# Attention and a gated feed-forward: loads of q and k for two head pairs at a time, output rows stored whole, and a new order

## The chip, the cores and the metric

The kernel runs on one core of a Trainium2 chip. The core has five engines that run programs of their own and meet at semaphores: TensorE (PE in the profile; its weight loads are listed apart as PEld), VectorE (DVE), ScalarE (ACT), GpSimd (POOL) and SyncE (SP), which here only issues DMAs. The metric is the device time of one execution in microseconds; times of a kernel are the median of several runs. A page of the profile and a trace show one more execution, instruction by instruction.

## What is computed

Attention with RMS-normalised q and k over 8 batches of 12 heads (sequence 448, head size 64), then for each batch a feed-forward block with a gate that comes from a convolution along the sequence:

```python
q_n, k_n = rmsnorm(q, g_q), rmsnorm(k, g_k)          # x / sqrt(mean(x*x) + 1e-6) * g
scores = np.matmul(q_n, k_n.transpose(0, 1, 3, 2)) / sqrt(64)
attn = np.exp(scores - scores.max(-1)); attn /= attn.sum(-1) + 1e-9
x = np.matmul(attn, v)                               # (8, 12, 448, 64) -> (8, 448, 768)
h = np.maximum(x @ w_in, 0.0)                        # w_in 768 x 1024
conv_out = sum(conv_w[k] * hp[:, k:k + S] for k in range(3))   # hp: h padded by one row
gate = 1.0 / (1.0 + np.exp(-conv_out))
out = (h * gate) @ w_out                             # w_out 1024 x 768
```

All inputs and outputs are float32. The large products are made of float16 parts: each operand is split into a high and a low half, and three products (high x high, high x low, low x high) are added up in a bank of PSUM.

## The kernel before

**Tiling.** The 96 heads are worked in 48 pairs (n = 0 to 47, six pairs make a batch). For a pair the q and k rows lie in a buffer `qk0`, `qk1` or `qk2` (`qkbuf`, L169): 128 partitions x (q, k) x 2 heads x 4 row blocks x 64 numbers. The steps of a pair are: `load_k` (L358, two DMAs) and `load_q` (L369, one DMA) from HBM; `square` (L375, on ScalarE as L378 or on POOL as L95); `square_sum` (VectorE); `rsqrt` (L406 to L440, on VectorE or POOL, for two pairs in one step from pair 2 on: `duo(n)` at L402 gives the first of the two and their number); `apply_rms` (`sq<-qk,st`, L95); then `qk_transpose` on TensorE (L494) or `x_turn` by DMA, and the split into halves; `scores` (L673, matmuls with 64 rows); `soft_max` and `soft_exp` (L688); the split of the probabilities into a high half (L83) and a low half, `p_lo` (`ph<-e,ph`, L95, on VectorE or POOL); `p_turn` (L726, DMA transposes issued by SyncE; the first ten pairs are turned on TensorE); `pv` (L824, weights of 64 columns). Row sums are turned by a small matmul (L755), stored to DRAM and loaded back as a broadcast (`rB`, L774), by which `x_scale` (L831) divides. v is split likewise: `v_hi`, and `v_lo` at L801, which only VectorE does. L83, L87, L89 and L95 are lines of helpers through which the steps copy, scale and combine.

**The feed-forward.** When a batch's six pairs are done, `in_part` (L898) multiplies x by w_in for each of 8 blocks of 128 hidden units, `in_relu`, `in_conv` (L926) and `in_gate` (L936) follow, the result is split into `gring` (NGR = 13 slots; with slots in the freed weight tiles NGS = 16), and `out_part` (L977) multiplies by w_out, per chunk of 128 rows (`ch`) and half of 384 columns (`half`). `out_evac` (L982) moves a half from PSUM into a tile of the pool "c", and `out_store` (L991) stores that half, 192 KB. The weights are split in the first 130 us, block by block: `rest` makes the low halves, on POOL with two instructions (L314, L315) or on VectorE with one (L317).

**Order.** Nothing runs in the order of the source. Every step is written as a function, planned at a time (`at(...)`, `plan_qk`, `plan_moe` ...), and at build time a list scheduler puts all steps of all engines in one order: `needs` says which steps must come before, `options` which engines may do a step and how long each takes, `takes` and `vacant` which tile it holds, and the numbers in `PH` (L20) set due times and priorities (`p_lo` for the step p_lo, `nl` for how many hidden blocks of the last batch start early, `nbulk` for how many large loads may be under way). So the choice of engine for a step (`on[...]`) comes out of it too. Where a step waits is decided by the semaphores that follow from this order.

Buffers (`BUFS`, L106): 3 of q and k, 12 of `x`, 3 of `c` (hidden values in conversion and output halves), 2 of `rB`, and 8 banks of PSUM shared by scores, transposes and matrix sums. The three buffers of q and k are single pairs: `load_k(n)` needs the normalisation of pair n - 3.

Of the kernel before, what the change touches and what calls it, by code (L numbers as in the profile page):

```python
# [20 lines left out]
    T0=11.0, N0=5, T=16.382, ti=26.404, si=4.968, so=8.766, hop=0.561, beta=0.03, wi0=-36.475,  # L21
    wi1=117.871, wo0=26.473, wo1=140.589, cw=-9.12, tg=-80.448, tl=37.151, ea=0.984, te=114.439,
    ep=0, hs=0, nf=3, adj=0.197, nz=8, ne=0, sc=5, tc=2, mc=9, p_qe=0.915, p_evac=0.829,
    p_hi=1.186, p_lo=6.193, p_rms=1.69, p_v=0.867, p_x=0.082, p_g=2.32, p_relu=0.547, p_cv=1.114,
    p_qz=0.74, p_ev=5.993, sp=0.148, nbulk=6, p_rs=0.05, p_sq=0.891, p_w=0.552, v0=-6.388, dg=7,
    n1=10, sw=0.0, nl=3, tj=-0.029, hk=0, pvs=1, pk=0.1, p_sa=0.167, p_ph=0.412, p_pl=0.72, nq=3,
    nk=92, p_qh=0.575, p_ql=0.384, tq=10.598, ti0=0.04, ti1=0.124, ti2=-0.224, ti3=0.742,
    ti4=0.066, ti5=-0.171, ti6=0.596, ti7=0.034, si0=0.995, si1=1.598, si2=1.683, si3=1.424,
    si4=1.633, si5=1.152, si6=1.198, si7=1.044, to0=0.237, to1=0.161, to2=-0.044, to3=0.013,
    to4=0.226, to5=-0.711, to6=-0.117, to7=0.325, so0=1.431, so1=1.535, so2=1.849, so3=1.519,  # L30
    so4=2.126, so5=1.521, so6=1.163, so7=0.964,
# [23 lines left out]
def tile_attention_moe(ctx: ExitStack, tc, q, k, v, g_q, g_k, w_in, conv_w, w_out, out):  # L55
# [41 lines left out]
    def move(e, dst, src):  # L97
# [9 lines left out]
        qkf=3, sq=2, st=2, qT=2, kT=2, qz=2, v=4, sst=6, e=2, PT=2, x=12, c=3,  # L107
        rB=2, vacc=2, vsc=4, cwb=3, s=PH["sc"], t=PH["tc"], m=PH["mc"], rd=2, rsum=2, rT=1, mx=10, ph=3, vp=2,
# [60 lines left out]
    qkbuf = [const.tile([P, 2, 2, 4, D], F32, name=f"qk{i}") for i in range(BUFS["qkf"])]  # L169
# [6 lines left out]
    NGR = 13  # L176
# [180 lines left out]

    def load_k(n):  # L358
        ring = rings.setdefault("qkf", Ring(BUFS["qkf"]))
        x = ring.put(("qkf", n), qkbuf[ring.count % BUFS["qkf"]])  # L360
        rows = slice(n * 2 * S, (n + 1) * 2 * S)
        src = kf[rows].rearrange("(h k) d -> h k d", h=2)
        for i, m in enumerate((4, 3)):
            queue("lk").dma_start(
                x[HALF[i], 1, :, :m],
                src[:, 256 * i : 256 * i + 64 * m].rearrange("h (p t) d -> p h t d", t=m),
            )

# [71 lines left out]
    def apply_rms(n, i):  # L440
# [5 lines left out]
            old("qkf", n)[:m, i], y.unsqueeze(3).to_broadcast([m, 2, NB, D]), ALU.mult,  # L446
# [96 lines left out]
    def plan_qk(n):  # L543
        s = base(n)
        lead = PH["tl"] if n else 60.0
        at(s - lead, load_k, n)
        at(s - lead, load_q, n)
# [434 lines left out]
    def out_evac(b, ch, half):  # L982
        sc = old("vsc", b - 1)[:, 5:6] if b % 2 == 1 and ch == 0 else old("vsc", b)[:, 4:5]
        o = new("c", ("o", b, ch, half), [P, S], F32)
        copy_scaled(
            on["out_evac", b, ch, half], o[:, :NO2], bank("m", ("o", b, ch, half))[:, :NO2], sc
        )

    def out_store(b, ch, half):
        row0 = out_place(b, ch)[1]  # L990
        queue("out").dma_start(  # L991
            outf[row0 : row0 + P, half * NO2 : (half + 1) * NO2],
            old("c", ("o", b, ch, half))[:, :NO2],
        )

    def plan_moe(b):
# [25 lines left out]
        for i, (ch, half) in enumerate(units):  # L1022
# [4 lines left out]
            at(u + so + 2.0, out_store, b, ch, half)  # L1027
# [17 lines left out]
    def prepare():  # L1045
# [705 lines left out]
```

## Time and profile before

| | us |
|---|---|
| three runs | 892.53, 888.18, 892.11 |
| median | 892.11 |
| the profiled execution: its time | 887.41 |
| the profiled execution: its span (first to last instruction) | 885.6 |
| mean granted clock of TensorE | 0.984 of full speed |

| engine | busy us | share of the span | instructions |
|---|---|---|---|
| TensorE, matmul | 817.3 | 92% | 5416 |
| TensorE, weight load (beside) | 417.8 | 47% | 5416 |
| VectorE | 721.8 | 81% | 1189 |
| ScalarE | 677.3 | 76% | 1474 |
| POOL | 603.0 | 68% | 744 |

A group of instructions is named by its line, engine, operation and tiles: `sq<-qk` is an instruction that reads q and k and writes the squares. In a list of single instructions the first number is the start in us from the span's begin, the second the duration, and in brackets stands the idle time of the engine before it with the instruction that ended it. All sums below are made against the profiled execution, 887.41, and then put on the median.

### The profile page before, as it was taken

To read this page: it belongs to the slowest core of one execution; us is meant where nothing else is said; L and a number is where in the kernel's file an instruction comes from. 1 tells how busy PE (TensorE), PEld (TensorE's weight loads), DVE (VectorE), ACT (ScalarE), POOL (GpSimd) and SP (SyncE) were. 2 spreads that over 40 slices of the span, in tenths; PEclk is the share of its full clock that TensorE was granted. 3 is DMA by queue.
4 is the path that set the end of the run, shared out by engine and by line. 5 is a ranking of instruction groups with operands and counts; after the bars stand their busy time and mean duration, and the time that the engine had idled before them with its cause. 6 is when DMAs were issued, how large, how long until landed. Compare 5 with 4: busy or idle time off the path is not lost.

```text
span 885.6 us, 16303 instructions
## 1 busy us (share of the span) xinstructions
PE 817.3 (92%) x5416; PEld 417.8 (47%) x5416; DVE 721.8 (81%) x1189; ACT 677.3 (76%) x1474; POOL 603.0 (68%) x744
## 2 busy tenths in 40 slices
PE   0588889999999799999999999998999999999998
PEld 0244444544444344455545554544455555555554
DVE  5889998889989998899888888989898788971330
ACT  1778878879988898888888878987688778783441
POOL 6238867668777977887878756887678868853120
PEclk9989999999999899999999999999899999999999
DMA  8936642128898888888998699979588888456101
GB/s 267 263 104 168 174 98 63 36 77 162 193 195 170 147 179 177 188 179 168 193 180 179 123 184 191 186 159 178 122 166 164 159 168 175 102 111 136 37 11 62
DMA packets 343585, 132.65 MB, mean 150 GB/s; under 512 B 303461, under 2 KB 341709, under 8 KB 342733
## 3 DMA queue, kind: packets, MB, share of 16 engines
q1 hardware_dynamic: 343500, 131.61, 70.3%
q8 instruction: 43, 0.70, 0.3%
q14 instruction: 42, 0.34, 0.1%
HBM read 58.22 MB, written 11.18 MB: 78 GB/s over the span
## 4 chain that ended last, share of the span: by engine, by line
PE 71%; DVE 15%; POOL 4%; ACT 4%; issue 4%; DMA 2%; SPq 1%; ACTq 0%; POOLq 0%; DVEq 0%
PE banks L977 21%; PE banks L898 20%; PE banks L673 10%; PE banks L824 9%; PE banks L494 4%; PE banks L815 3%; PE banks L735 3%; DMA qk<-in_q_dram 1%; DVE st L395 1%; ACT e L688 1%; DVE ph L95 1%; POOL ph L95 1%; PE banks L755 1%; DVE vp L801 1%; DVE kT L530 1%
## 5 line engine op out<-in xcount | busy, mean ns | idle before, releaser
L95 POOL TENSOR_TENSOR ph<-e,ph 128x768 f16<-128x768 f32 (+3 forms) x272 | 256.9, 966 | 72.3 <-ACT ph L83 56.7
L898 PE MATMUL banks<-x,wi 128*128 128x448 f16 x1152 | 253.8, 356 | 0.7 <-ACT PT L83 0.7
L977 PE MATMUL banks<-wo,gring 128*128 128x384 f16 (+1 forms) x1056 | 210.4, 328 | 0.0
L898 PEld LDWEIGHTS <-wi 128*128 128x128 f16 x1152 | 109.0, 99 | 102.3 <-issue 19.4
L977 PEld LDWEIGHTS <-gring 128*128 128x128 f16 (+1 forms) x1056 | 100.8, 99 | 74.1 <-issue 16.1
L83 ACT CAST ph<-e 128x1024 f16<-128x1024 f32 (+1 forms) x139 | 129.4, 931 | 5.3 <-DMA PT<-ph 3.5
L673 PE MATMUL banks<-kT,qT 64*128 64x448 f16 x864 | 107.2, 362 | 8.2 <-DVE qT L532 4.7
L95 POOL TENSOR_TENSOR sq<-qk,st 112x512 f32<-112x512 f32 (+1 forms) x85 | 94.4, 1127 | 23.1 <-DVE st L417 8.2
L824 PE MATMUL banks<-PT,vp 128*64 128x448 f16 (+1 forms) x836 | 98.2, 365 | 4.2 <-DVE c_(1_6_3089 L936 3.1
L494 PE MATMUL banks<-ident,sq 128*128 128x128 f32 (+1 forms) x364 | 61.0, 280 | 26.1 <-POOL sq L95 20.3
L395 DVE TENSOR_REDUCE st<-sq 128x16 f32<-128x1024 f32 x48 | 58.0, 1209 | 16.7 <-ACT sq L378 16.6
L494 PEld LDWEIGHTS banks<-ident,sq 128*128 128x128 f32 (+1 forms) x364 | 43.9, 144 | 53.1 <-POOL sq L95 23.2
L95 POOL TENSOR_TENSOR x<-rB,x 128x448 f16<-128x448 f32 x48 | 53.2, 1109 | 22.1 <-ACT x L83 20.8
L824 PEld LDWEIGHTS <-vp 128*64 128x64 f16 (+1 forms) x836 | 41.8, 110 | 55.0 <-issue 35.3
L673 PEld LDWEIGHTS <-qT 64*128 64x128 f16 x864 | 35.1, 95 | 64.1 <-issue 36.2
L735 PE MATMUL banks<-ident,e 128*128 128x128 f32 x280 | 45.4, 291 | 12.7 <-ACT PT L83 5.7
L378 ACT ACTIVATE sq<-qk 128x1024 f32<-128x1024 f32 x41 | 43.3, 1056 | 11.7 <-DMA qk<-in_q_dram 11.4
L831 DVE TENSOR_TENSOR rB<-banks,rB 128x448 f32<-128x448 f32 x48 | 29.7, 618 | 26.7 <-PE banks L824 20.7
L541 POOL COPY qz<-qT 64x128 f16<-64x128 f16 x86 | 32.4, 377 | 25.0 <-DVE qT L532 17.7
L977 PE MATMUL banks<-wo,wi 128*128 128x384 f16 (+1 forms) x192 | 46.9, 326 | 0.0
L735 PEld LDWEIGHTS banks<-ident,e 128*128 128x128 f32 x280 | 32.4, 146 | 29.7 <-ACT PT L83 10.6
L83 ACT COPY PT<-banks 128x512 f32<-128x512 f32 x63 | 36.0, 582 | 9.9 <-PE banks L735 9.5
(1152 smaller groups left out, 1688.8 us busy)
## 6 DMA issues: line engine op xcount, KB each, us to landing
qk<-in_q_dram SPq DMA_DIRECT2D x48, 224.0 KB
rB<-rd SPq DMA_DIRECT2D x96, 112.0 KB
qk<-in_k_dram SPq DMA_DIRECT2D x48, 128.0 KB
wo<-in_moe_w_in_dram SPq DMA_DIRECT2D x6, 1024.0 KB
v<-in_v_dram SPq DMA_DIRECT2D x24, 256.0 KB
gring<-in_moe_w_out_dram SPq DMA_DIRECT2D x8, 768.0 KB
qk<-in_k_dram SPq DMA_DIRECT2D x48, 96.0 KB
v<-in_v_dram SPq DMA_DIRECT2D x24, 192.0 KB
```

The lines of the kernel that those rows point to most:

```text
L83: (nc.scalar.copy if e == "ACT" else elementwise(e).tensor_copy)(dst, src)
L95: elementwise(e).tensor_tensor(dst, a, b, op=op)
L378: nc.scalar.activation(sq, old("qkf", n), AF.Square)
L395: nc.vector.tensor_reduce(old("st", m)[:, 0, n - m].rearrange("p i s -> p (i s)"), old("sq", n).rearrange("p i h t d -> p (i h t) d")[..., ...
L494: nc.tensor.transpose(ps[:, t * w : t * w + m], x[:m, t], ident[:m, :m])
L541: e.tensor_copy(z[HALF[h], :, HALF[h]], old("qT", n)[HALF[h], :, t0 : t0 + 64])
L673: nc.tensor.matmul(ps[u][:, :S], lhs, kt[r, w], start=(i == 0), stop=(i == 2))
L735: nc.tensor.transpose(ps[:, kt * P : (kt + 1) * P], e[:, k0 : k0 + P], ident)
L824: nc.tensor.matmul(ps[HALF[h], :S], v[:m, w, h, c % 4], pt[:m, c, h * S : (h + 1) * S], start=(i == 0), stop=(i == len(PV7) - 1),)
L831: nc.vector.tensor_tensor(t, bank("m", ("v", n))[:, :S], t, op=ALU.mult)
L898: nc.tensor.matmul(ps[:, :S], wi[:, wl, c, fc * P : (fc + 1) * P], old("x", b * NP + c)[:, xl], start=(i == 0), stop=(i == 3 * NP - 1),)
L977: nc.tensor.matmul(ps[p0 : p0 + m, :NO2], g, wo[:, wl, fc, half * NO2 : (half + 1) * NO2], start=(i == 0), stop=(i == 3 * NFC - 1),)
```

## The change

The three buffers of a single pair become two buffers of two pairs. Pairs 0 and 1 are still loaded singly; from pair 2 on one `load_k` and one `load_q` bring two pairs, 23 times. The other steps of a pair take their half of the buffer (`qk(n)`). The load of pairs n and n + 1 needs the normalisation of pairs n - 4 and n - 3.

An output chunk is gathered in one tile "o" of 768 columns (a pool with one buffer) and stored once, 384 KB.

Other buffers: `x` 12 to 10, `c` 3 to 2, `rB` 2 to 1, `gring` 13 to 12 slots. `nl` goes from 3 to 4, so that four hidden blocks of the last batch are worked while its last chunks of x are still made, and the step that writes a slot of `gring` now needs all chunks of the older batch that read the slot. The numbers of `PH` are set anew, and with them the order on all engines and the choice of engine of some steps.

```diff
-    T0=11.0, N0=5, T=16.382, ti=26.404, si=4.968, so=8.766, hop=0.561, beta=0.03, wi0=-36.475,
+    T0=11.0, N0=5, T=16.382, ti=26.404, si=4.968, so=8.925, hop=0.57, beta=0.03, wi0=-36.475,
...
-        qkf=3, sq=2, st=2, qT=2, kT=2, qz=2, v=4, sst=6, e=2, PT=2, x=12, c=3,
-        rB=2, vacc=2, ...
+        qkf=2, sq=2, st=2, qT=2, kT=2, qz=2, v=4, sst=6, e=2, PT=2, x=10, c=2, o=1,
+        rB=1, vacc=2, ...
...
-    qkbuf = [const.tile([P, 2, 2, 4, D], F32, name=f"qk{i}") for i in range(BUFS["qkf"])]
+    qkbuf = [const.tile([P, 2, 2, 2, 4, D], F32, name=f"qk{i}") for i in range(BUFS["qkf"])]
...
-    NGR = 13
+    NGR = 12
...
+    def qk_rows(x, n):
+
+        w = duo(n)[1]
+        a, b = n * 2 * S, (n + w) * 2 * S
+        return x[a:b].rearrange("(h k) d -> h k d", h=2 * w), slice(n % 2, n % 2 + w)
+
     def load_k(n):
         ring = rings.setdefault("qkf", Ring(BUFS["qkf"]))
-        x = ring.put(("qkf", n), qkbuf[ring.count % BUFS["qkf"]])
-        rows = slice(n * 2 * S, (n + 1) * 2 * S)
-        src = kf[rows].rearrange("(h k) d -> h k d", h=2)
+        if n % 2 == 0:
+            ring.put(("qkf", n // 2), qkbuf[ring.count % BUFS["qkf"]])
+        src, u = qk_rows(kf, n)
...
+    def qk(n):
+
+        return old("qkf", n // 2)[:, :, n % 2]
...
-        o = new("c", ("o", b, ch, half), [P, S], F32)
...
-    def out_store(b, ch, half):
+        if half == 0:
+            new("o", (b, ch), [P, DM], F32)
+        o = old("o", (b, ch))[:, half * NO2 : (half + 1) * NO2]
+        copy_scaled(on["out_evac", b, ch, half], o, bank("m", ("o", b, ch, half))[:, :NO2], sc)
+
+    def out_store(b, ch):
         row0 = out_place(b, ch)[1]
-        queue("out").dma_start(
-            outf[row0 : row0 + P, half * NO2 : (half + 1) * NO2],
-            old("c", ("o", b, ch, half))[:, :NO2],
-        )
+        queue("out").dma_start(outf[row0 : row0 + P], old("o", (b, ch)))
...
             pb = back(b, a[1], NGS, NFC)[0]
-            yield "out_part", pb, 3 if pb % 2 else 2, 1, 3 * NFC - 4, 4
+            for ch in range(4 if pb % 2 else 3):
+                for u in range(2):
+                    yield "out_part", pb, ch, u, 3 * NFC - 4, 4
```

What the new order looks like at three places. First SyncE's program around the loads of pairs 34 and 35, before; `qk1` takes pair 34 and `qk2` pair 35, `PT_30` to `PT_32` are the turned probabilities of pairs 30 to 32, `rd` and `rB` the row sums:

```order
L726 DMA_TRANSPOSE PT_30_5854<-ph2_73 128x7x128
L364 DMA qk1_77<-in_k_dram 64x2x256
L364 DMA qk1_77<-in_k_dram 64x2x192
L371 DMA qk1_77<-in_q_dram 112x8x64
L774 DMA rB_30_6006<-rd_30_5946 64x448 x2
...
L768 DMA rd_31_6154<-rT_31_6130 7x128
L364 DMA qk2_78<-in_k_dram 64x2x256
L364 DMA qk2_78<-in_k_dram 64x2x192
L726 DMA_TRANSPOSE PT_32_6178<-ph1_72 128x14x128
L371 DMA qk2_78<-in_q_dram 112x8x64
```

and now:

```order
L738 DMA_TRANSPOSE PT_30_5795<-ph2_73 128x7x128
L370 DMA qk1_77<-in_k_dram 64x4x256
L370 DMA qk1_77<-in_k_dram 64x4x192
L786 DMA rB_30_5945<-rd_30_5894 64x448 x2
L738 DMA_TRANSPOSE PT_31_5958<-ph0_71 128x14x128
L377 DMA qk1_77<-in_q_dram 112x16x64
```

Both pairs' rows are now asked for where pair 34's alone were, and the second group of loads, behind the sums of pair 31, is gone.

Second, TensorE around the products with v of pair 20 (weight loads and repeats are left out at the marks), before:

```order
L824 MATMUL banks_66<-PT_20_3750,vp_20_3770 64x448
...
L494 MATMUL banks_66<-ident_69,sq_22_3664 128x128 x3
...
L673 MATMUL banks_66<-kT_21_3709,qT_21_3728 128x448
...
L494 MATMUL banks_66<-ident_69,sq_22_3664 128x112 x4
...
L824 MATMUL banks_66<-PT_20_3750,vp_20_3770 64x448
...
L898 MATMUL banks_66<-x_14_2905,wi32_82 128x448
```

and now:

```order
L505 MATMUL banks_66<-ident_69,sq_22_3638 128x112 x4
...
L910 MATMUL banks_66<-x_14_2877,wi32_81 128x448
...
L685 MATMUL banks_66<-kT_21_3672,qz1_79 128x448
...
L836 MATMUL banks_66<-PT_20_3739,vp_20_3618 64x448
...
L910 MATMUL banks_66<-x_15_3054,wi32_81 128x448
```

The transposes of pair 22 and scores of pair 21, which stood between two parts of the product, now stand ahead of it, and the product is in one piece.

Third, POOL in the first 100 us, between the halves of pair 5 (`sq_5`) and its part of the rsqrt of pair 6 (`st_6`); `wi32` is w_in, `x_1` and `x_2` the results of pairs 1 and 2. Before:

```order
L95 TENSOR_TENSOR qk2_78<-sq_5_511,qk2_78 112x512
L314 TENSOR_SCALAR wi32_82<-wi32_82,wsc_86 128x1024
L315 TENSOR_TENSOR wi32_82<-wi32_82 128x1024
L95 TENSOR_TENSOR x_2_803<-rB_2_729,x_2_803 128x448
L423 TENSOR_SCALAR st_6_826<-st_6_826 128x32
```

and now:

```order
L95 TENSOR_TENSOR qk0_76<-sq_5_468,qk0_76 112x512
L314 TENSOR_SCALAR wi32_81<-wi32_81,wsc_85 128x1024
L315 TENSOR_TENSOR wi32_81<-wi32_81 128x1024
L95 TENSOR_TENSOR x_1_679<-rB_1_613,x_1_679 128x448
...
L95 TENSOR_TENSOR sq_7_809<-qk1_77 128x1024
L95 TENSOR_TENSOR x_2_825<-rB_2_738,x_2_825 128x448
...
L434 TENSOR_SCALAR st_6_815<-st_6_815 128x32
```

At the two marks stand a second and a third pair of L314 and L315 and small copies: POOL does three blocks of w_in here (two in the whole program before, one of them earlier than this) and the square of pair 7, all ahead of the rsqrt of pair 6.

## Rows read from the trace of the kernel before

**Rows 1.** Windows: start:end, length, busy us of each engine, clock, DMA share, GB/s.

```profile
0.00:140.00 140.00, 94.58 (x556) 47.73 (x557) 119.98 (x204) 95.95 (x216) 87.38 (x113) 0.97 0.66 175
80.00:100.00 20.00, 16.73 (x104) 8.18 (x104) 19.93 (x24) 18.11 (x41) 17.97 (x13) 1.00 0.61 163
140.00:660.00 520.00, 500.65 (x3349) 251.73 (x3348) 466.11 (x762) 436.75 (x955) 393.27 (x488) 0.98 0.79 160
300.00:320.00 20.00, 16.40 (x120) 8.27 (x121) 19.21 (x36) 16.77 (x36) 16.57 (x18) 0.83 0.65 142
620.00:640.00 20.00, 19.52 (x107) 8.74 (x103) 15.77 (x23) 12.36 (x28) 13.42 (x18) 0.86 0.63 127
640.00:660.00 20.00, 18.28 (x109) 9.08 (x110) 18.55 (x30) 16.73 (x35) 12.15 (x18) 0.91 0.83 174
660.00:882.00 222.00, 222.00 (x1515) 118.37 (x1513) 135.68 (x224) 144.01 (x304) 122.36 (x145) 1.00 0.55 113
```

The engines stand in the order PE, PEld, DVE, ACT, POOL, with the number of instructions in brackets.

**Rows 2.** Timeline of TensorE, 363 to 371 us: start, duration, instructions.

```profile
364.34 0.73 PE L898 MATMUL banks<-x,wi 128*128 128x448 f16 x3
365.00 1.82 PE L824 MATMUL banks<-PT,vp 128*64 128x448 f16 x16
...
369.22 0.74 PE L898 MATMUL banks<-x,wi 128*128 128x448 f16 x3
369.80 0.33 PE L977 MATMUL banks<-wo,gring 128*128 128x384 f16 x1
```

**Rows 3.** Groups by line and shape: count, then busy us, mean ns, idle before.

```profile
L317 DVE SCALAR_TENSOR_TENSOR wi<-wi,wsc 128x1024 f16<-128x1024 f32 x4 | 5.5, 1366 | 0.0
L317 DVE SCALAR_TENSOR_TENSOR wo<-wo,wsc 128x768 f16<-128x768 f32 x4 | 4.3, 1064 | 0.2 <-ACT wo L309 0.2
...
L95 POOL TENSOR_TENSOR sq<-qk 128x1024 f32<-128x1024 f32 x7 | 13.9, 1985 | 8.1 <-PE banks L494 6.7 <-issue 1.3
...
L314 POOL TENSOR_SCALAR wo<-wo,wsc 128x768 f32<-128x768 f32 x4 | 8.9, 2214 | 3.7 <-ACT wo L309 3.7
...
L315 POOL TENSOR_TENSOR wo<-wo 128x768 f16<-128x768 f32 x4 | 6.6, 1646 | 0.3
L314 POOL TENSOR_SCALAR wi<-wi,wsc 128x1024 f32<-128x1024 f32 x2 | 6.4, 3210 | 0.6 <-ACT wi L309 0.6
...
L315 POOL TENSOR_TENSOR wi<-wi 128x1024 f16<-128x1024 f32 x2 | 4.3, 2132 | 0.2
```

**Rows 4.** Timeline of TensorE at the transposes of pair 6.

```profile
108.02 0.75 PE L494 MATMUL banks<-ident,sq 128*128 128x128 f32 x4 [1.59 <-POOL sq L95]
```

**Rows 5.** Timelines around the load of q of pair 35: DMA, ScalarE, TensorE.

```profile
545.94 4.88 DMA qk<-in_q_dram
550.92 1.06 ACT L378 ACTIVATE sq<-qk 128x1024 f32<-128x1024 f32 x1 [3.63 <-DMA qk<-in_q_dram]
...
554.01 0.27 PE L755 MATMUL banks<-ident,rsum 128*7 128x128 f32 x1 [1.38 <-DVE rsum L752]
```

**Rows 6.** Line L801: min/median/max ns; then timelines of 609 to 621 us.

```profile
L801 DVE SCALAR_TENSOR_TENSOR vp<-v,vsc,vp x38: 732/747/4728, 193.9 to 790.2; 128x512 f16<-128x512 f32 x38
...
611.64 4.63 DVE L801 SCALAR_TENSOR_TENSOR vp<-v,vsc,vp 128x512 f16<-128x512 f32 x1
611.72 4.01 POOL L95 TENSOR_TENSOR ph<-e,ph 128x768 f16<-128x768 f32 x4
...
619.49 0.38 PE L755 MATMUL banks<-ident,rsum 128*7 128x128 f32 x1 [3.04 <-DVE rsum L752]
```

**Rows 7.** Timeline of 300 to 303 us, VectorE and TensorE.

```profile
300.75 1.61 DVE L432 TENSOR_TENSOR st<-st 128x32 f32<-128x32 f32 x1 [0.40 <-POOL st L430]
...
302.94 2.45 PE L824 MATMUL banks<-PT,vp 128*64 128x448 f16 x12 [3.09 <-DVE c_(1_6_3089 L936]
```

**Rows 8.** The end: timeline of ScalarE; then DMA, 882 to 886 in 40 slices.

```profile
882.19 0.58 ACT L87 ACTIVATE c_('o'_7_3_1_9926<-banks,vsc 128x384 f32<-128x384 f32 x1 [3.32 <-PE banks L977]
...
GB/s 0 0 0 0 0 0 0 0 0 0 0 0 0 0 0 0 169 384 399 338 399 231 46 0 0 0 0 0 0 0 0 0 0 0 0 0 0 0 0 0
```

More of the change, by code (lines that the diff above doesn't have):

```diff
@@ L369, in load_q @@
     def load_q(n):
-        rows = slice(n * 2 * S, (n + 1) * 2 * S)
+        src, u = qk_rows(qf, n)
         queue("lq").dma_start(
-            old("qkf", n)[:PB, 0], qf[rows].rearrange("(h t p) d -> p h t d", h=2, t=NB),
-        )
+            old("qkf", n // 2)[:PB, 0, u].rearrange("p u h t d -> p (u h) t d"),
+            src.rearrange("h (t p) d -> p h t d", t=NB),
+        )
+    def qk(n):
+        return old("qkf", n // 2)[:, :, n % 2]
     def square(n):
@@ L377, in square @@
         if on["square", n] == "ACT":
-            nc.scalar.activation(sq, old("qkf", n), AF.Square)
+            nc.scalar.activation(sq, qk(n), AF.Square)
         else:
-            binary("POOL", sq, old("qkf", n), old("qkf", n), ALU.mult)
+            binary("POOL", sq, qk(n), qk(n), ALU.mult)
     def square_half(n):
@@ L545, in plan_qk @@
         lead = PH["tl"] if n else 60.0
-        at(s - lead, load_k, n)
-        at(s - lead, load_q, n)
+        if duo(n)[0] == n:
+            at(s - lead, load_k, n)
+            at(s - lead, load_q, n)
         at(s - 24.0, square, n)
@@ L1026, in plan_moe @@
             at(u + so, out_evac, b, ch, half)
-            at(u + so + 2.0, out_store, b, ch, half)
+            if half:
+                at(u + so + 2.0, out_store, b, ch)
     def load_g(i):
@@ L1167, in needs @@
             for i in range(2):
-                m = n - BUFS["qkf"]
-                yield ("x_turn" if turned(m, i) else "apply_rms"), m, i
-            yield "load_q", n - 1
+                for m in range(duo(n)[1]):
+                    m += n - 2 * BUFS["qkf"]
+                    yield ("x_turn" if turned(m, i) else "apply_rms"), m, i
+            yield "load_q", duo(n - 1)[0]
         elif name == "load_q":
@@ L1173, in needs @@
         elif name == "square":
-            yield "load_q", n
+            yield "load_q", duo(n)[0]
             for i in range(2):
@@ L1391, in needs @@
             yield "out_scales", b
+            if a[2]:
+                yield "out_evac", b, a[1], 0
         elif name == "out_store":
-            yield "out_evac", *a
+            for u in range(2):
+                yield "out_evac", *a, u
     def back(n, g, i, m=NS):
@@ L1431, in options @@
             keep_cw=lambda: [dve(0.2), act(0.25)],
-            load_k=lambda: [dma("lk", 0.41, 2)],
-            load_q=lambda: [dma("lq", 1.36)],
+            load_k=lambda: [dma("lk", 0.41 * duo(a[0])[1], 2)],
+            load_q=lambda: [dma("lq", 1.36 * duo(a[0])[1])],
             square=lambda: [act(1.06), pool(1.9)],
@@ L1476, in options @@
             out_evac=lambda: [act(0.58), dve(0.6)],
-            out_store=lambda: [dma("out", 0.65)],
+            out_store=lambda: [dma("out", 1.3)],
             sum_transpose=lambda: [pe(0.12)],
@@ L1524, in takes @@
             return "c", [(None, ("in_lo", *a[:2]))]
-        if name == "out_evac":
-            return "c", [(None, ("out_store", *a))]
+        if name == "out_evac" and not a[2]:
+            return "o", [(None, ("out_store", *a[:2]))]
         return None, []
@@ L1586, in ends @@
             return done[p] + LAT["DMA" if d else f]["DMA" if dma else e]
-        if tag == "c":
+        if tag in "co":
             old_users = held[tag][-BUFS[tag] :]
```

35 lines of the change are left out of this document (16 added, 19 removed).

## The prediction

> **What bounds the kernel now.** I first cut the span into stretches by the view that gives every engine's busy time in a window [rows 1]. In 660–882 us TensorE is busy 222.00 of 222.00 us: nothing can be gained there except by making its own work shorter. In 140–660 it is busy 500.65 of 520, so 19.35 us are idle. In 0–140 it is busy 94.58, so 45.42 are idle, and VectorE with 119.98 is the fullest engine; in 80–100 VectorE has 19.93 of 20 and POOL 17.97. Then I followed the idle times of 140–660 back, by the timelines of single stretches. They have two sorts of cause. One is a late load: the q rows of pair 35 take 4.88 us to land, ScalarE's square behind them idles 3.63, and 3 us later TensorE idles 1.38 on a result of VectorE [rows 5]. The other is an element-wise step on VectorE that stretches while POOL works: L801 has a median of 747 ns, but at 611.64 it took 4.63 us, beside a low-half step of POOL that began at 611.72 with four instructions of 4.01 us; 8 us later TensorE idles 3.04 us [rows 6]. The same at 300.75: L432 takes 1.61 us behind POOL's half of the same pair, and TensorE idles 3.09 us at 302.94 [rows 7].
>
> Such a gap costs more than itself. The granted clock is 0.83 in 300–320, 0.86 in 620–640 and 0.91 in 640–660, each time after the gap, against 1.00 in stretches without one [rows 1]: between the two levels of 1.2 and 2.4 GHz, some of these stretches ran at the lower. At 20 us each, (0.17 + 0.14 + 0.09) x 20 = 8.0 us of full-speed time lost, with the gaps 3.09 + 3.04 = 6.1: 14.1 us hang on two places, about 7 us each.
>
> So the time is TensorE's work, plus a startup that VectorE sets, plus a few accidents between engines. The change removes no matmul; its reach is in the order, the startup, the accidents and the last store.
>
> **The change part by part**, against the profiled execution's own 887.41 us (0.53% under the median of 892.11).
>
> *TensorE's order.* The matmuls are the same in number and shape. What the order does is to set kinds apart or together: 64-row scores, 64-column PV and full 128 x 128 tiles. In the listings, shape changes along TensorE's program go from 320 to 302. A change has a small price: three in_part matmuls followed by a PV hold TensorE from 364.34 to 365.00, 0.66 us, the same three followed by an out_part of the same shape from 369.22 to 369.80, 0.58 [rows 2]. 18 x 0.08 = 1.4 us, all on the path as far as TensorE is saturated. Ends: 0 to -1.8. I take **-1.4**.
>
> *Startup.* Three `rest` steps of the weights go from VectorE to POOL: one of w_in (1.37 us) and two of w_out (1.06 each), 3.5 us off the fullest engine; POOL gets 2 x L314 + L315: 3.21 + 2.13 and twice 2.21 + 1.65, together 13.1 us [rows 3]. In the stretch 80–100 POOL has only 2 us left [rows 1]. In the order, POOL now has a third weight step and a whole square (1.99 us by [rows 3]) ahead of its part of the rsqrt of pair 6. And TensorE's transposes of pair 6 waited 1.59 us on POOL at 108.02 already before [rows 4]. So VectorE gives up to 3.5 back, and POOL may take as much: it has 7.3 us more ahead of that point (5.3 + 2.0), against the waits that it had there. Ends: -4 and +3. I take **-1.0**, nearer to VectorE's row, since it is the engine at 19.93 of 20.
>
> *Loads of two pairs.* Per two pairs, three DMA issues instead of six; SyncE has 97 issues fewer in all, and none of them was on the path. The odd pair's rows now come with the even one's, so a wait like that of pair 35 (3.63 on ScalarE, 1.38 on TensorE [rows 5]) has no place any more: its load is issued a whole pair earlier. In return the even pair waits for a transfer of twice the bytes, by [rows 5] up to 4.88 us more if the transfer is as slow as there, and the load itself must wait until both pairs of its buffer have been normalised. The even pairs' loads stood some microseconds ahead of their squares. One full gap like [rows 5] with a little low clock behind it is 2 us; there is one clear case in the trace. Ends: -4 (two such) and 0 (another wait is next behind it). I take **-2.0**.
>
> *Which engine does which element-wise step.* POOL gets nine more squares, 9 x 1.985 = 17.9 us, and the 13.1 us of `rest` [rows 3]; four more low halves of P and thirteen fewer casts about cancel. That is 31 us more on POOL, of which 18 lie in 140–660, where it is busy 393.27 of 520 [rows 1]. VectorE gets lighter by a few microseconds: fewer two-operand steps (16 to 12 low halves of P, 126 to 116 rsqrt steps). Fewer back-to-back runs of P's low halves stand on POOL now (28 to 22 in the listing). Whether the two places of 7 us recur is a matter of microseconds of alignment: with a new order they can vanish (-14.1), stay (0), or others come (+7 each). I take **-1.5**, a little under a quarter of one place, as fewer such pairs meet on VectorE's side but POOL is fuller.
>
> *The store of 768 columns.* Earlier stores are covered. Behind the last one nothing is: TensorE's last bank is moved out from 882.19 to 882.77, and the bytes of the store behind it move in some 6 to 7 slices of 0.1 us, 0.6 us of them at full rate [rows 8]. Twice the bytes after the last eviction: **+0.6** (0 if longer rows move faster, +1.2 if the whole is issued slower).
>
> *Fewer buffers and the earlier start of the last batch's chunks.* x 12 to 10, c 3 to 2, one rB and one o buffer: in the order the releasing step stands well ahead of the reuse for all of them; should an eviction wait for the previous store it has 4 us for it. The ring of gate values has one slot fewer, and the last batch's chunk 7 now waits until the second-last batch's output chunks are all read; the two out_part groups of about 0.67 us between cover it. Since TensorE has no idle time in 660–882 [rows 1], a wait here would be seen in full. **+0.5** (0 to +3).
>
> Sum: -1.4 - 1.0 - 2.0 - 1.5 + 0.6 + 0.5 = -4.8: 882.6 against 887.41. On the median: 892.11 - 4.8 = **887.3 us**.
>
> A rule of the Trainium skill speaks against the change. In "SBUF — State Buffer", section "Who interferes with whom", it says that VectorE and GpSimd share one pair of ports as an exclusive lock, and that a VectorE instruction with two SBUF inputs contends with a GpSimd one that reads SBUF, the later one being blocked fully. The trace agrees: 4.63 us against a median of 747 ns [rows 6]. Taken by itself, with more POOL reads beside VectorE, the rule would give the time of rival C below.
>
> **The rivals.**
> *B, the accidents go.* Both places of [rows 6, 7] vanish or shrink, for the low halves meet less often, and no new ones come. Half to all of 14.1 us is gained instead of 1.5; with the middle, -10, the sum is -13: **879**. With one place, 882. I take 881 as its time. For: VectorE's two-operand steps fall in number. Against: POOL is fuller.
> *C, slower: POOL blocks VectorE elsewhere.* POOL's 18 us more in 140–660 are nine squares of 1.985 us, each a two-operand read just where VectorE normalises the pair before. If a square holds up a VectorE step that TensorE waits for, as in [rows 6], a place costs about 7 us with the clock behind it, or 3 without. It decides from one such place with its clock on: -4.8 + 1.5 + 7 = +3.7; two give -4.8 + 1.5 + 14 = +10.7, two without the clock -4.8 + 1.5 + 6 = +2.7. Between these I take +6: **898**. For: a fuller POOL. Against: the squares can stand where VectorE has no two-operand step, and one was hit at only two places of some hundred.
> *D, nothing.* Startup is handed from VectorE to POOL (+1 to +3 instead of -1.0), the even pairs' longer load eats the odd ones' gain (0 instead of -2.0): -4.8 + 2 + 2 = -0.8: **891.5**.
>
> **How the numbers follow.** What a measurement of this kernel can tell from no change is about 0.5%, 4.46 us: faster is under 887.65, slower over 896.57. The forecast (A, 887.3, from 883 to 891) gets 0.45, of which 0.27 faster and 0.18 the same, since it stands just on the bound; B 0.20, faster; D 0.18, of which 0.17 the same and 0.01 slower; C 0.17, slower. Faster 0.47, same 0.35, slower 0.18. The range is to leave out 0.2: from 879, which keeps most of B, to 898, C's middle.
>
> **What would show it.** In the trace after: TensorE's idle time in 0–140 against 45.42 (startup; under 45 if VectorE was the bound, over 47 if POOL now is); idle time in 140–660 against 19.35, and the windows of 20 us with a clock under 0.95 (300–320, 620–640 and 640–660 here; by B none of this kind, by C at least as many at new places); L813, the low half of v, with a maximum near its median by B; squares of odd pairs without idle time on a load; the last bytes 0.6 us later behind the last eviction. TensorE not full in 660–882 would break the sum from another side: then a thinner ring or the earlier start of the last chunks costs more than 0.5. If in_part triples behind a PV still take 0.66 us and others 0.58, the price of a shape change was right; the sum of TensorE's order then shows in its busy time.

## The result and the profile after

| | before | after |
|---|---|---|
| median beside each other, us | 891.55 (4 runs, 888.18 to 892.53) | 880.43 (4 runs, 879.89 to 881.50) |
| ratio, 95% interval | | 0.9883 [0.9855, 0.9912] |
| a second series (29 and 12 runs), ratio | | 0.9930 [0.9896, 0.9963] |
| span of the profiled execution, us | 885.6 | 879.1 |
| TensorE busy, us | 817.3 | 816.9 |
| POOL busy, us | 603.0 | 632.7 |

The change makes the kernel faster, by 1.2% in one series and 0.7% in the other. The two profiled executions differ by 6.5 us. Ratios leave out executions more than 1.5% above the fastest of their kernel, in the second series seven of the 29 of the kernel before (893.63 to 897.00 us) and one more of the kernel after (1364.16 us, at a mean granted clock of 0.564).

The windows of the kernel after, with the columns of [rows 1]:

```profile
0.00:140.00 140.00, 98.87 (x560) 50.55 (x561) 115.89 (x196) 98.34 (x220) 89.57 (x117) 0.96 0.70 175
140.00:660.00 520.00, 505.23 (x3404) 254.86 (x3402) 475.13 (x796) 438.21 (x960) 424.89 (x503) 0.99 0.82 162
280.00:300.00 20.00, 14.46 (x93) 6.60 (x90) 19.32 (x25) 14.81 (x35) 15.13 (x19) 0.91 0.64 123
300.00:320.00 20.00, 16.02 (x106) 7.21 (x106) 18.76 (x40) 16.03 (x34) 16.20 (x19) 0.74 1.00 185
620.00:640.00 20.00, 19.85 (x130) 10.23 (x128) 18.88 (x32) 18.18 (x40) 15.94 (x17) 1.00 1.02 192
640.00:660.00 20.00, 20.00 (x136) 9.97 (x134) 18.06 (x33) 16.51 (x35) 17.69 (x25) 1.00 0.89 177
740.00:760.00 20.00, 17.74 (x121) 9.34 (x120) 17.38 (x24) 14.71 (x34) 16.12 (x25) 1.00 0.64 136
```

Against [rows 1], 620 to 660 is full and at 1.00 now, but 300 to 320 is worse than before (0.74 against 0.83), and a hole stands in 740 to 760, where TensorE had been full.

Where the time went can be read more closely than by windows. Both programs hold the same matmuls; so for a time of the kernel before one can ask when the kernel after had done as much work (each kind of step counted by its duration at full clock in the trace of before; another way of counting moves single entries by up to 0.8). The lead of the kernel after, in us:

| at (us of the kernel before) | 140 | 200 | 280 | 340 | 540 | 560 | 600 | 660 | 740 | 800 | end |
|---|---|---|---|---|---|---|---|---|---|---|---|
| lead | 1.8 | 2.8 | 3.6 | -1.2 | -1.2 | 0.3 | 1.2 | 9.1 | 9.5 | 7.0 | 7.1 |

Four pieces make it: about +3 by 200 us, -4.8 at 280 to 340, +7.9 at 600 to 660 and -2.5 at 740 to 800, with +1.5 at 540 to 560; the last store takes 0.6 back. In the kernel before two low halves of v were held at 600 to 660, the one of [rows 6] and one that is the maximum of its first row; its line, and TensorE's wait behind it:

```profile
634.97 4.73 DVE L801 SCALAR_TENSOR_TENSOR vp<-v,vsc,vp 128x512 f16<-128x512 f32 x1
...
641.72 0.72 PE L494 MATMUL banks<-ident,sq 128*128 128x128 f32 x4 [2.19 <-DVE c_(5_0_7185 L936]
```

The two losses in the timelines of the kernel after, VectorE, POOL and TensorE:

```profile
279.69 3.57 DVE L552 COPY qz<-qT 64x128 f16<-64x128 f16 x1
280.03 2.04 POOL L95 TENSOR_TENSOR sq<-qk,st 128x512 f32<-128x512 f32 x2
282.04 1.17 POOL L95 TENSOR_TENSOR ph<-e,ph 128x384 f16<-128x384 f32 x2
288.29 0.35 PE L685 MATMUL banks<-kT,qT 64*128 64x448 f16 x1 [3.08 <-DVE c_(1_4_2847 L948]
...
749.32 4.78 DVE L95 TENSOR_TENSOR gring<-c_(6_1_8554,gring 128x448 f16<-128x448 f32 x1
750.00 4.39 POOL L95 TENSOR_TENSOR ph<-e,ph 128x768 f16<-128x768 f32 x4
754.69 2.51 PE L836 MATMUL banks<-PT,vp 128*64 128x448 f16 x22 [2.26 <-DVE c_(6_2_8655 L948]
```

They are the pattern of [rows 6] at new places: a small step of VectorE (a copy whose 17 calls have a median of 0.25 us; a low half whose four other calls on VectorE took 0.38 to 1.60 us) beside a train of POOL instructions, and 5 to 9 us later TensorE waits on VectorE. So the accidents did not go away, they moved: the forecast's rivals B and C both happened, at different places. TensorE waits more than 0.8 us at seven places between 140 us and the end in either trace; its idle time in 140 to 660 is 14.8 us instead of 19.35.

Not every block costs something. A low half of v is held in the kernel after as well (the maximum of L813 is 3.78 us, the median 0.74):

```profile
590.67 3.78 DVE L813 SCALAR_TENSOR_TENSOR vp<-v,vsc,vp 128x512 f16<-128x512 f32 x1
591.27 1.04 POOL L95 TENSOR_TENSOR gring<-c_(4_6_6605,gring 128x448 f16<-128x448 f32 x1
```

From 586 to 606 us TensorE's longest wait is 0.29 us: nothing that it needed soon stood behind this step.

The end of the kernel after, ScalarE, SyncE and the DMA view of 874 to 879 us in 40 slices, beside [rows 8]:

```profile
875.09 0.58 ACT L87 ACTIVATE o_(7_3_9804<-banks,vsc 128x384 f32<-128x384 f32 x1 [3.27 <-PE banks L989]
875.70 0.33 SPq L1003 DMA_DIRECT2D out_dram<-o_(7_3_9804  x1
...
GB/s 0 0 0 0 0 0 0 0 0 0 0 0 0 0 0 0 0 0 0 0 295 418 393 393 393 418 393 393 50 0 0 0 0 0 0 0 0 0 0 0
```

From the last eviction's start to the end of the span it is 4.0 us, 3.4 before: the whole row's bytes move in some 8 slices of 0.125 us.

The squares, by line (ScalarE, then POOL), beside the POOL row of [rows 3]:

```profile
L389 ACT ACTIVATE sq<-qk 128x1024 f32<-128x1024 f32 x32 | 33.6, 1051 | 5.3 <-DMA qk<-in_q_dram 4.7 <-PE banks L505 0.6
...
L95 POOL TENSOR_TENSOR sq<-qk 128x1024 f32<-128x1024 f32 x16 | 30.9, 1932 | 8.0 <-PE banks L505 3.9 <-DMA PT<-ph 1.8 <-issue 1.3
```

### The profile page after: what moved, and what is told of

It reads as the page before. It is cut to its first block, busy times and chain, and to the rows that moved or that the text cites. A ratio compares the mean times of both kernels' runs of the same rounds, so it can differ in the third digit from the quotient of the medians.

```text
span 879.1 us, 16158 instructions
## 1 busy us (share of the span) xinstructions
PE 816.9 (93%) x5416; PEld 419.9 (48%) x5416; DVE 720.2 (82%) x1204; ACT 672.5 (76%) x1468; POOL 632.7 (72%) x760
## 4 chain that ended last, share of the span: by engine, by line
PE 72%; DVE 14%; POOL 4%; ACT 3%; issue 3%; DMA 2%; SPq 1%; DVEq 0%; POOLq 0%; ACTq 0%
PE banks L910 22%; PE banks L989 21%; PE banks L685 10%; PE banks L836 9%; PE banks L505 4%; PE banks L827 3%; PE banks L747 2%; POOL sq L95 1%; DMA qk<-in_k_dram 1%; DVE ph L95 1%; POOL ph L95 1%; ACT e L700 1%; DVE st L406 1%; PE banks L767 1%; DVE gring L95 1%
## 5 line engine op out<-in xcount | busy, mean ns | idle before, releaser
L95 POOL TENSOR_TENSOR ph<-e,ph 128x128 f16<-128x128 f32 (+3 forms) x280 | 264.5, 967 | 56.7 <-ACT ph L83 40.1
L83 ACT CAST ph<-e 128x1024 f16<-128x1024 f32 (+1 forms) x147 | 136.9, 931 | 3.8 <-DMA PT<-ph 1.7
L95 POOL TENSOR_TENSOR sq<-qk,st 112x512 f32<-112x512 f32 (+1 forms) x83 | 92.3, 1130 | 9.6 <-DVE st L428 4.1
L747 PE MATMUL banks<-ident,e 128*128 128x128 f32 x280 | 47.4, 302 | 10.4 <-ACT PT L83 5.0
L989 PE MATMUL banks<-wo,wi 128*128 128x384 f16 (+1 forms) x192 | 49.7, 327 | 0.0
L685 PE MATMUL banks<-kT,qz 128*128 128x448 f16 x144 | 38.1, 376 | 2.8 <-DVE c_(1_6_3033 L948 2.8
L83 ACT CAST x<-rB 128x448 f16<-128x448 f32 x44 | 24.7, 561 | 20.3 <-DVE rB L843 20.0
```

The source lines that it names most:

```text
L83: (nc.scalar.copy if e == "ACT" else elementwise(e).tensor_copy)(dst, src)
L95: elementwise(e).tensor_tensor(dst, a, b, op=op)
L685: nc.tensor.matmul(ps[u][:, :S], lhs, kt[r, w], start=(i == 0), stop=(i == 2))
L747: nc.tensor.transpose(ps[:, kt * P : (kt + 1) * P], e[:, k0 : k0 + P], ident)
L989: nc.tensor.matmul(ps[p0 : p0 + m, :NO2], g, wo[:, wl, fc, half * NO2 : (half + 1) * NO2], start=(i == 0), stop=(i == 3 * NFC - 1),)
```

## The experiments

Each keeps one of the two orders and changes single steps in it. Three series were run, each on one chip, with the kernel before beside them (medians 884.65, 885.59 and 885.55 us). Where several kernels are compared, the ratios to the kernel before are, and across two series only that. Where the traces of two kernels of the same order are compared, each matmul is set against the same one of the other.

**Which part of the gain are the loads?** The kernel before, its order untouched, with the new loads:

```diff
     def load_k(n):
+        if duo(n)[0] != n:
+            return
...
+    BUFS.update(x=10, rB=1)
```

> The kernel before with its order of steps kept on every engine; only q and k come for two pairs at a time into two buffers of two pairs (where the even pair's load stood; the odd pair's own load is gone), x has 10 and rB 1 buffer. Stores stay halves. Theory 'order' (the 11 us are in the new order: a startup about 2 us shorter, and another set of places where VectorE is held up by POOL): the same as before within 3 us, 889 to 892; pair 35's idle of 1.38 us on TensorE at 554 goes. Rival 'loads' (the merged, earlier loads are the gain): 880 to 886.

Measured: 883.12 us (nine runs; a tenth took 2046.62), ratio 0.9983 [0.9949, 1.0016]. Pair 35's wait at 554 us is gone (between the traces +1.6 us at 540 to 560), and the others stay. In this execution the same order brought the same accidents at the same steps; timelines of VectorE in this kernel, beside [rows 6]:

```profile
608.10 4.63 DVE L816 SCALAR_TENSOR_TENSOR vp<-v,vsc,vp 128x512 f16<-128x512 f32 x1
...
630.15 4.73 DVE L816 SCALAR_TENSOR_TENSOR vp<-v,vsc,vp 128x512 f16<-128x512 f32 x1
```

So the loads by themselves are worth some 1.5 us, too little for these runs to tell from nothing. The rest came with the new order and what goes with it (buffers, stores, the engines of some steps). The whole trace of this run is 4.9 us shorter than the trace of before: besides the 1.6 it gained 1.0 at the startup and 1.3 at 610 to 630, with both low halves held as before. Two executions of one order can differ by so much.

**What does a block cost?** The kernel before with the two low halves of v moved, and, in another run, the changed kernel with its two blocked steps given to POOL:

```diff
+    on["q_middle", 37, 1] = on["q_middle", 38, 1] = "POOL"
+    behind(("q_middle", 37, 1), ("q_middle", 37, 0))
+    behind(("q_middle", 38, 1), ("q_middle", 38, 0))
+    behind(("v_lo", 36), ("out_evac", 4, 0, 0))
+    behind(("v_lo", 37), ("in_conv", 5, 1, 1))
+    behind(("v_load", 22), ("v_lo", 37))
```

(`behind(step, other)` puts a step right behind another in the order; the load of v goes along because it takes the buffer that the step reads.)

> The kernel before, with two steps taken out of the way of POOL: the low halves of v of pairs 36 and 37, which took 4.63 and 4.73 us instead of 0.75, stand later on VectorE, where POOL had nothing to do, and two copies of 64 columns (pairs 37 and 38) go from VectorE to POOL. Theory 'blocks': TensorE's idle time of 3.04 us at 619.49 and 2.19 at 641.72 and the low clock after them (0.86, 0.91) go: 6 to 9 us less, ratio 0.990 to 0.993. Rival 'no slack' (VectorE is full anyway, so another wait comes next): 0 to 2 us less.

```diff
+    on["q_middle", 16, 1] = on["in_lo", 6, 1] = "POOL"
+    behind(("q_middle", 16, 1), ("q_middle", 16, 0))
```

> The changed kernel with two steps moved from VectorE to POOL, in the same order: the copy of 64 columns of pair 16, which took 3.57 us instead of 0.25 at 279.69, and the low half of hidden block (6, 1), which took 4.78 us instead of about 0.7 at 749.32. Theory 'blocks': the idle times of TensorE behind them (3.08 at 288.29, part of 2.00 and 2.84 at 300 to 305, 2.26 at 754.69) and the low clock in 300 to 320 (0.74) go: 6 to 11 us less than the changed kernel, ratio to before 0.975 to 0.981. Rival 'next wait': 0 to 3 us less, ratio 0.985 to 0.988.

Measured: the old order 883.72 us, 0.9973 [0.9930, 1.0016], its runs spread from 876.70 to 892.09; the new order 874.06 us, 0.9867 [0.9797, 0.9937]. The old order's ratio can't be told from nothing. Its trace shows the mechanism: the two steps took 1.07 and 1.32 us, and from 600 to 646 us TensorE gained 8.4 us on the kernel before, as expected. Then 4.0 of them were lost again, to a high half of v at the next place:

```profile
643.83 3.79 DVE L89 TENSOR_SCALAR vp<-v,vsc 128x512 f16<-128x512 f32 x1
...
648.80 1.06 PE L673 MATMUL banks<-kT,qT 64*128 64x448 f16 x5 [2.04 <-DVE kT L530]
```

So "no slack" was right as well. The whole of this execution, 890.37 us, shows no gain for another reason: it lost 6.3 us at 312 to 318, at a place that was not touched (one execution, one of the two longest, so for the median this is a guess, which the next experiment tests):

```profile
313.16 4.41 DVE L541 COPY qz<-qT 64x128 f16<-64x128 f16 x1
...
319.00 0.58 PE L210 MATMUL banks<-mx,ones 1*128 1x1 f32 x2 [4.03 <-DVE mx L205]
319.51 0.53 PE L977 MATMUL banks<-wo,carry 128*64 128x384 f16 x1
```

The same copy in the profiled execution of the kernel before, same order:

```profile
312.12 0.74 DVE L541 COPY qz<-qT 64x128 f16<-64x128 f16 x1
```

In the new order the two moves gained 3.6 us at 280 to 340 and 1.9 at 740 to 800 on the kernel after, 5.7 us at the end between the two traces: just under what was expected, since two idle times behind the first place stayed (2.75 and 2.83 us). The ratio, of four runs, lies in the rival's range (0.985 to 0.988), but that range was reckoned from the first series' 0.9883; from the second series, below (0.9930), the gain is 4 to 6 us, between the two theories. Windows of 280 to 320 and 740 to 760 with the two steps on POOL:

```profile
280.00:300.00 20.00, 13.72 (x100) 6.76 (x99) 19.07 (x33) 17.32 (x40) 16.48 (x21) 0.96 0.71 139
300.00:320.00 20.00, 18.40 (x134) 8.77 (x135) 19.00 (x36) 17.14 (x39) 17.58 (x18) 0.78 1.12 196
740.00:760.00 20.00, 19.58 (x132) 10.18 (x130) 16.54 (x25) 16.99 (x37) 17.21 (x25) 1.00 0.61 129
```

**Does the copy of pair 18 decide between the runs of the kernel before?**

```diff
+    on["q_middle", 18, 1] = "POOL"
+    behind(("q_middle", 18, 1), ("q_middle", 18, 0))
```

> The kernel before with one step moved from VectorE to POOL: the second copy of 64 columns of pair 18. In one execution of that order it took 0.74 us (at 312.12), in another 4.41 us (at 313.16), and TensorE then idled 4.03 us at 319. Theory 'two outcomes': that place decides between the runs of the kernel before at 880 to 886 us (15 of 29 in one series) and those at 889 to 897 (14 of 29); without it the upper ones go, median 880 to 884, ratio 0.990 to 0.996. Rival: the spread has another cause and stays; ratio 0.998 to 1.002.

Measured: 882.91 us, 0.9964 [0.9933, 0.9996], between the two theories' ratios; twelve runs from 878.90 to 886.52, while of the 29 runs of the kernel before beside it twelve are above 887, up to 894.90. On POOL the two copies take 0.63 us together:

```profile
308.71 0.63 POOL L541 COPY qz<-qT 64x128 f16<-64x128 f16 x2 [1.80 <-DVE qT L532]
```

The upper group is gone with the copy. The long copy itself was seen in one execution of the old order only; that it is what lifts the kernel before's upper runs is the likeliest reading, not more. (In the first experiment, with the copy on VectorE, one of nine runs was above 887, and five of 19 of the kernel before beside it: too few to speak for or against.) In the new order the long copy shows up twice more below.

This trace also shows that an order doesn't fix which step is held. VectorE's second low half of v is through at once, and the copy behind it, 0.19 us in the trace of before, is held:

```profile
630.94 0.79 DVE L801 SCALAR_TENSOR_TENSOR vp<-v,vsc,vp 128x512 f16<-128x512 f32 x1
...
632.77 3.05 DVE L541 COPY qz<-qT 64x128 f16<-64x128 f16 x1
```

**The changed kernel once more, and a version that beats both.**

> The changed kernel itself once more, beside the runs of the kernel before, which spread from 879 to 891 us. Theory 'the profile' (two executions of like luck differ by 6.5 us: 885.6 and 879.1 of span): ratio 0.990 to 0.994. Rival 'the medians' (11 us): ratio 0.986 to 0.990.

Measured: ratio 0.9930 [0.9896, 0.9963], in the range of the first theory; eleven runs lie from 876.71 to 885.18. (Its trace is of the twelfth, the one of 1364.16 us, and is not used.) The two series together say 6 to 11 us, and the traces 6.5. It is the kernel before that differs between them: the kernel after has medians of 880.43 and 879.39 us, the kernel before 891.55 and 885.59, and its first four runs all lie above 887, where 31 of the 77 later ones do. Whether that was the draw or the chip can't be told.

```diff
+    on["q_middle", 16, 1] = on["q_middle", 18, 1] = on["in_lo", 6, 1] = "POOL"
+    behind(("q_middle", 16, 1), ("q_middle", 16, 0))
+    behind(("q_middle", 18, 1), ("q_middle", 18, 0))
```

> The changed kernel with three steps moved from VectorE to POOL: the second copies of pairs 16 and 18 and the low half of block (6, 1). Theory 'places': the gain of the first and the third (5.7 us between two traces) stays, and the copy of pair 18, which took 3.20 us in the run with the old engines for the weights, can't cost 4 us any more: 870 to 875, ratio 0.981 to 0.988. Rival 'next wait': 877 or more, ratio above 0.990.

Measured: 875.44 us, 0.9896 [0.9857, 0.9936], between the two theories and no better than with two moves; in the trace with two moves this copy took 0.59 us, so that there was nothing to gain. Then the first and the third of these moves, without the copy of pair 18, and besides the reciprocal of pair 16's sums ahead of a reduction over v, and the last chunk stored in halves:

```diff
+    behind(("sum_inverse", 16), ("sum_add", 16))
+    behind(("v_bound", 11), ("in_conv", 1, 6, 2))
+    order[order.index(("out_store", 7, 3))] = "out_store", 7, 3, 1
+    order.insert(order.index(("out_evac", 7, 3, 0)) + 1, ("out_store", 7, 3, 0))
```

> The changed kernel with the copy of pair 16 and the low half of block (6, 1) on POOL, and besides: on VectorE the reciprocal of pair 16's sums stands ahead of a reduction over v of 1.20 us, which goes three steps later; the last chunk is stored in two halves. Theory 'places': the gains of the two moves (4.2 us in 280 to 320, 2.3 near 750) and 1.5 to 3 us more at the idle time of 2.75 us before TensorE's turn of those sums, and 0.6 at the end: 7 to 10 us less than the changed kernel. Rival 'next wait': at most 4 us less.

Measured: 874.33 us, 0.9876 [0.9837, 0.9914], beside 0.9930 for the changed kernel in the same series: some 5 us better, between the two theories. That is what two moves gave; the traces don't show that the rest added to it. The idle time of 2.75 us before the turn of the sums went to 1.08, and TensorE's next long wait grew from 2.83 to 6.30 us; timeline of VectorE and TensorE:

```profile
291.59 0.28 PE L767 MATMUL banks<-ident,rsum 128*7 128x128 f32 x1 [1.08 <-ACT e L700]
...
295.90 2.00 DVE L428 SCALAR_TENSOR_TENSOR st<-st 128x32 f32<-128x32 f32 x2
...
299.49 1.28 PE L685 MATMUL banks<-kT,qz 128*128 128x448 f16 x3 [6.30 <-DVE c_(1_6_3033 L948]
```

There "next wait" was right: VectorE is full in this stretch (19 of 20 us in the windows above), and only its long blocks can be taken out, not its work.

**The startup.** The changed kernel with the weights' low halves where the kernel before made them:

```diff
+    for w, c, e in (("in", 2, "DVE"), ("in", 4, "POOL"), ("in", 5, "DVE"), ("out", 2, "DVE"), ("out", 7, "DVE")):
+        on["rest", w, c] = e
```

> The changed kernel in its own order; the low halves of the weights are made by the engines of the kernel before (w_in blocks 2 and 5 and w_out blocks 2 and 7 on VectorE again, w_in block 4 on POOL). Theory 'VectorE bounds the startup': 1 to 3.5 us more than the changed kernel, TensorE's idle time in 0 to 140 us up from 41 by that. Rival 'POOL bounds it as well' (forecast case D): no change, or 1 to 3 us less.

Measured: 884.51 us, 0.9968 [0.9933, 1.0003], 3 to 5 us worse than the changed kernel in the same series, and not for the expected reason: at 140 us TensorE is where it was (0.2 us behind between the traces, busy 99.03 in 0 to 140 against 98.87). The 4 us are lost at 300 to 320, to the copy of pair 18 again:

```profile
313.63 3.20 DVE L552 COPY qz<-qT 64x128 f16<-64x128 f16 x1
...
319.69 0.38 PE L210 MATMUL banks<-mx,ones 1*128 1x1 f32 x2 [4.54 <-DVE mx L205]
```

**POOL's squares.** The change gave POOL nine more; here eleven of its sixteen go to ScalarE.

```diff
+    for n in range(7, NPAIR):
+        if n not in (9, 13, 25, 31, 45, 47):
+            on["square", n] = "ACT"
```

> The changed kernel in its own order with eleven squares (pairs 7, 15, 17, 19, 21, 23, 29, 33, 35, 41, 43) on ScalarE (1.06 us each) instead of POOL (1.9 to 2.0). Theory: POOL's squares hang on no wait of TensorE, and ScalarE has little room: 0 to 3 us more than the changed kernel. Rival C of the forecast (a fuller POOL holds up VectorE): 3 us or more less.

Measured: 885.01 us, 0.9991 [0.9961, 1.0020], by the ratios of two series 5 us worse than the changed kernel. Taking 21 us of squares off POOL doesn't help, which speaks against rival C in the form that it was given (a square holds up VectorE). It doesn't show that squares hold up nothing: in this trace, 1.1 us behind the kernel after at the end, the copy of pair 18 took 3.20 us as well. How much of the 5 us is ScalarE's work is open.

**The stores.** Each half stored by itself:

```diff
-    def out_store(b, ch):
+    def out_store(b, ch, half):
...
+        cols = slice(half * NO2, (half + 1) * NO2)
```

> The changed kernel in its own order, but each half of an output chunk is stored by itself as soon as it is moved out: 28 DMA issues more, and only 192 KB behind the last eviction. Theory: 0.6 us less at the end (the forecast's term), nothing else. Rival (28 issues of about 0.6 us more on SyncE hold up loads or transposes): 1 to 4 us more.

Measured: 879.59 us, 0.9952 [0.9921, 0.9983], the changed kernel's time within what can be told. The last eviction starts at 873.69 and the span ends at 877.0: 3.3 us instead of 4.0, as forecast; the 28 issues cost nothing that shows.

**The form and the place of the loads.** Two runs of the changed kernel, which keep its buffers of two pairs but fill them by DMAs of one pair: at the same place, and with the odd pair's where the kernel before had it (behind the same DMA in SyncE's program, by steps put into the order).

```diff
     def qk_rows(x, n):
-        w = duo(n)[1]
+        w = 1
```

> The changed kernel in its own order, but the two pairs of a load come by six DMAs of one pair each instead of three of two, at the same place in SyncE's program. Theory (what counts is when the odd pair's rows are there, not the size of a DMA): 0 to 2 us more than the changed kernel. Rival (fewer issues on SyncE are the gain): 4 us or more above it.

> The changed kernel in its own order, but each pair's q and k loaded singly; the odd pair's load stands in SyncE's program where it stood in the kernel before (behind the same DMA), the even one's where it stands now. Theory 'order': 0 to 2 us more than the changed kernel, ratio 0.988 to 0.991. Rival 'loads' (an odd pair's rows that come with the even one's are worth more than the 2.0 us forecast): 4 us or more lost, ratio above 0.993.

Measured: at the same place 881.74 us, 0.9959 [0.9931, 0.9988], 2.6 us behind the kernel after between the traces, a little over the theory's 0 to 2 and under the rival's 4; late 937.86 us, 1.0596 [1.0536, 1.0656]. Neither theory of the second run had that. POOL's squares, by line:

```profile
L95 POOL TENSOR_TENSOR sq<-qk 128x1024 f32<-128x1024 f32 x16 | 30.9, 1931 | 66.2 <-DMA qk<-in_q_dram 57.2 <-issue 4.1 <-DVE sst_(44_2_8569 L691 3.1
```

57.2 us of waits for q, and the time is 57 us longer. In the new order an odd pair's square stands early on POOL, next to the even one's on ScalarE, which needs both pairs' rows early, by one DMA or by two; if the rows come late, all of POOL's queue stands behind it, the low halves of P among it. The early rows are little gain over the old order, but the new order could not stand without them.

## Why the prediction was right, and where it was off

The forecast was 887.3 us, 4.8 under the median of before; measured were 880.43 us and, by the two series, 11 and 6 us less. The direction and the range (879 to 898) held. The size was between 1.3 and 2.3 times the forecast. By its steps, between the two traces:

- **TensorE's order, -1.4.** Too large. Where TensorE is full in both traces and nothing else happens (660 to 740) the lead grows by 0.4 us, and from 340 to 540 by nothing. The price of a change held: three in_part matmuls followed by scores or a PV take 0.66 to 0.67 us in the median in both traces, followed by an out_part 0.57. What failed is "all on the path": counted over all matmuls by 64 rows, 64 columns and full tiles, the changes fall from 517 to 498, but 15 of these 19 lie before 340 us, where TensorE waits for others; in 340 to 540 and from 660 to the end there are 225 before and 226 after.
- **Startup, -1.0.** TensorE's idle time in 0 to 140 is 41.1 us instead of 45.4, the lead 1.8 us at 140 and 2.8 at 200, inside the term's range, but the reason given for it falls: with the weights' steps back on their old engines the lead at 140 is unchanged. The traces of kernels with the old order differ from each other by up to 2.6 us at 140, and the kernel with four moves leads the kernel after by 3.6 us there, where the two are alike, so that the gain itself can't be told from the runs' spread. That POOL would take back what VectorE gave did not happen either.
- **Loads of two pairs, -2.0.** Right: 1.6 us at 540 to 560 in the old order with new loads, 1.5 between the two traces, by the very wait of [rows 5]. What it missed is that they carry the order (57 us if the odd rows come late).
- **Which engine does what, -1.5.** The two places of [rows 6, 7] were taken as one coin. They were two: the one at 611 and 635 went (+7.9), the one at 300 got worse (-4.8), and one came at 749 (-2.5). The sum, +0.6, is close to the forecast, and near nothing only because they cancel; that is luck. The price of 7 us a place was too high for a single block: 7.9 to 8.4 for the two low halves of v together, of which the forecast had seen one, 3.6 for the copy of pair 16, 1.9 to 2.5 for the block at 749, which had no lower clock behind it, and nothing for the one at 590.67.
- **The last store, +0.6.** Right: 4.0 us instead of 3.4 behind the last eviction.
- **Fewer buffers and the earlier last chunks, +0.5.** Nothing: from 800 us to the end the lead is 7.0 and 7.1.

The terms between the traces come to 6.5 us, 1.7 more than forecast. The step that failed by more is the last one, from the trace to the median: "on the median: 892.11 - 4.8". The profiled execution of before was 0.53% under the median, and the prediction took that as a constant to carry over; the kernel after's was 0.05% over its median, and in the later series the kernel before has medians of 884.65 to 885.59, under its profiled execution. From these, 4.8 us less is 880 to 881, about where the kernel after lies. But the runs of before were spread, and a spread has places too: the copy that took 0.74 us in that trace took 4.41 in another, and with it on POOL the kernel before's upper runs were gone. A median can hold such a price where the trace doesn't show it. That this is the whole of the difference between the two series is not shown.

(Rival D's sum gives 891.3, not 891.5, which changes nothing.) Of the chances, 0.47 for faster was low, but the time came out at rival B's (881) by a way that was half B and half C. The rule of the Trainium skill that was weighed there ("SBUF — State Buffer", "Who interferes with whom") names the contention that the traces show for steps with two inputs: 4.63 and 4.73 us for the low halves of v before, 4.78 for the low half at 749 after. It says less than happened, since such a step stayed held through several POOL instructions (last section), and of the copies, which read one tile, the part weighed there doesn't speak. What it was used for, that more POOL reads mean more lost time, holds for VectorE and not for the kernel: POOL did 30 us more, what VectorE's steps took over the median of their kind (by operation and shape) went from about 71 us to 74, and the time still fell, since it counts only where TensorE waits for it.

## What to carry to other kernels

In a schedule where two engines share a resource, price a place by the step that is hit and who waits for it some microseconds later, not by how busy the engines are; and expect a new order to deal such places anew, some gone and some new. When runs of one kernel differ by more than the effect that is forecast, find in the trace the step that can go either way before a difference is carried from one execution to a median. A small shared-resource step that precedes a wait of the bounding engine is worth moving to the other engine: two such moves gave some 5 us here, nearly as much as the whole change by its second series. Expect the next full engine to take a part back.

## What the runs showed of the hardware

A block can outlast the POOL instruction that it meets. The copy of pair 18 started 0.34 us into a POOL instruction in the one execution and was through 0.74 us later, when that had ended, though POOL's next one followed without a gap; in the other it started 0.78 us into the same one and was held through the five that followed, 4.41 us. POOL's timeline in the second:

```profile
312.38 1.03 POOL L95 TENSOR_TENSOR x<-rB,x 128x448 f16<-128x448 f32 x1
313.38 2.02 POOL L95 TENSOR_TENSOR ph<-e,ph 128x768 f16<-128x768 f32 x2
315.36 1.02 POOL L95 TENSOR_TENSOR wo<-c_(1_7_3156,wo 128x448 f16<-128x448 f32 x1
316.35 1.17 POOL L95 TENSOR_TENSOR ph<-e,ph 128x384 f16<-128x384 f32 x2
```

The copy ended at 317.57, with POOL's train at 317.52. Nor must it be the end of the train: with the weights' low halves on their old engines the same copy (313.63, 3.20 us) ended at 316.83, while POOL went on to 319.01, and the next step of VectorE was held in its turn:

```profile
313.87 1.02 POOL L95 TENSOR_TENSOR x<-rB,x 128x448 f16<-128x448 f32 x1
314.87 1.03 POOL L95 TENSOR_TENSOR sq<-qk,st 112x512 f32<-112x512 f32 x1
315.87 3.14 POOL L95 TENSOR_TENSOR ph<-e,ph 128x384 f16<-128x384 f32 x4
316.85 2.18 DVE L898 TENSOR_TENSOR vsc<-vsc,wsc 128x1 f32<-128x1 f32 x1
```

What decides whether VectorE gets its turn between two POOL instructions was not tried.
